# Two taps in one VectorE product, and a scaling moved to ScalarE, in the last phase of an SSM-convolution and gated-MLP training step

## The chip, the cores and the metric

The kernel runs on one core of a Trainium2 chip. The metric is device time in microseconds of one execution; lower is better. Of the kernel before, three runs were timed and one more was profiled.

## The reference

The forward pass normalizes x (2048 rows of 512), and adds three things: x itself, a long convolution gated by xn, and a bilinear MLP. The outputs are the forward result and all gradients:

```python
xn = (x - mean) / sqrt(var + 1e-5)
k_shift = sum(k_pad[:, t:t+S] * shift_k[:, 3 - t] for t in range(4))
kv = k_shift * v
y = irfft(rfft(kv) * rfft(ssm_k)) + kv * ssm_D
out_0 = x + xn * y + (xn @ w_gate * (xn @ w_up)) @ w_down
```

Three of the outputs matter here. `out_0` is the forward result. `out_1` is the gradient of x: with dxn the gradient that reaches xn, it is `rstd * (dxn - mean(dxn) - xn * mean(dxn * xn)) + grad_out`. `out_2` is the gradient of k, four shifted copies of the gradient of k_shift, each times one tap of shift_k, summed.

## The kernel before, in words

The 2048 rows lie as 128 partitions times 16 rows, so a block of two rows per partition is a tile of 128 x 2 x 512. The first phases do the MLP forward and backward by chunks of 256 rows, and the convolution as a staged Fourier transform through DRAM buffers. The last phase starts at about 315 us. Its main loop is `dw()` (line 1020): for each of eleven blocks of 128 hidden columns, TensorE turns the hidden values round (`hid_t`, line 846), and forms the weight gradients (`pd`, line 1002, and `pu`, line 1038). ScalarE copies the results out of PSUM: `nath` and `natd` from the transposes, `og` and `od` from the products. PSUM has three buffers of two banks (pool `ps2`, shared by pt, pu, pq, pk, po) and two small ones (pool `ps1`).

Between the steps of `dw()` four side jobs advance, each by its own start and step (line 1165): `inv_y` (the last inverse transform, which yields y and the gradient of k_shift, `dks`), `dsk_gram` (the tap gradient: TensorE products `pk`, VectorE masks `kd`), `inv_dk` (the gradient of ssm_k: `po`, `o5t`, which needs four loads `g` from DRAM, line 785) and `ew`, which runs the list `tail`.

`tail` holds, for b from 0 to 7, `final(b)` and one step later `bwd(b - 1)`. `final(b)` (line 1104) loads the next block `bb`, then writes `out_0` (o: a product, line 1112, a sum, line 1113, and the store, line 1114), and the norm gradient: `e` (line 1116), `dxn` with its two sums (lines 1120 and 1121), the two means (1122, 1123), `dxn + xn * m2` (1126), the scaling `e = dxn * rstd + m1` (1127), the sum with grad_out (1128) and the store of `out_1` (1129). All of it is on VectorE, and the stores are in SyncE's queue. `bwd(b)` (line 1083) writes `out_2`: four products with one tap each (1091 and 1093) and three sums (1094), on VectorE, and a store (1095).

Buffers: pool `c2` has one buffer for each name and `c2b` has two. So `o`, `e` and `dxn` have one buffer, which is written again one call later; `dk` and `bb` have two. `tk`, the temporary of `bwd`, shares the buffer of `dxn` (`tag="dxn"`). `dxn` is float32, 4 KB a partition; `tk` is bfloat16, 2 KB.

What sets the order: the code is traced, and a planner then writes the order of each engine's queue. It takes the place in the trace as an instruction's rank and its own table of costs for when inputs are there; blocks in `tc.high_priority(offset=SOON)` get a rank 300 earlier. On the chip each engine and each DMA queue takes its instructions in that order, and each waits for its inputs and for the readers of the buffer that it writes. Almost all loads and stores of this phase are issued by SyncE's one queue.

Of the kernel before, what the change touches and what calls it, by code (L numbers as in the profile page):

```python
# [8 lines left out]
BF = mybir.dt.bfloat16  # L9
F32 = mybir.dt.float32  # L10
I32 = mybir.dt.int32
ALU = mybir.AluOpType
ACTF = mybir.ActivationFunctionType
# [5 lines left out]
D = 512  # L19
F = 1376  # L20
R = 16
P = 128
# [168 lines left out]
def kernel(  # L191
# [24 lines left out]
    nc = tc.nc  # L216
    from concourse.masks import make_identity

    def nat(ap):
        return ap.rearrange("(p r) d -> p r d", r=R)  # L220
# [5 lines left out]
    o0_n = nat(out_0[0])  # L226
# [35 lines left out]
    skb = const.tile([P, 4, D], BF, name="skb")  # L262
    mv = const.tile([P, R, 2], F32, name="mv")
    rstd = const.tile([P, R], F32, name="rstd")
# [618 lines left out]
    for tag in mainit:  # L883
        if tag == "wa":
            wa_es.close()
            c1 = ctx.enter_context(tc.tile_pool(name="c1", bufs=1, reuse_waits="tile"))
            xnC = c1.tile([P, R, D], BF, name="xnC")
# [17 lines left out]
    c2 = ctx.enter_context(tc.tile_pool(name="c2", bufs=1, side="right", reuse_waits="tile"))  # L905
    yC = c2.tile([P, R, D], BF, name="yC")
    dks = c2.tile([P, R + 3, D], BF, name="dks")
    s1 = c2.tile([P, R], F32, name="s1")
    s2 = c2.tile([P, R], F32, name="s2")
    m1 = c2.tile([P, R], F32, name="m1")  # L910
# [172 lines left out]
    def bwd(b):  # L1083
        rb = slice(2 * b, 2 * b + 2)
        dk = c2b.tile([P, 2, D], BF, name="dk")
        t = c2.tile([P, 2, D], BF, name="tk", tag="dxn")
        for j in range(4):
            src = dks[:, 2 * b + j:2 * b + j + 2, :]
            w = skb[:, j:j + 1, :].to_broadcast((P, 2, D))
            if j == 0:  # L1090
                nc.vector.tensor_tensor(dk[:], src, w, op=ALU.mult)
            else:
                nc.vector.tensor_tensor(t[:], src, w, op=ALU.mult)  # L1093
                nc.vector.tensor_tensor(dk[:], dk[:], t[:], op=ALU.add)
        nc.sync.dma_start(o2_n[:, rb, :], dk[:])

    FL = {}
# [1 line left out]
    def load_fin(b):  # L1099
        bb = c2b.tile([P, 2, 2, D], BF, name="bb")  # L1100
        nc.sync.dma_start(bb[:], BX[:, 2 * b:2 * b + 2, :, :])
        FL[b] = bb

    def final(b):
        if b + 1 < 8:
            load_fin(b + 1)
        bb = FL.pop(b)
        rb = slice(2 * b, 2 * b + 2)
        tt = nc.vector.tensor_tensor
        stt = nc.vector.scalar_tensor_tensor  # L1110
        o = c2.tile([P, 2, D], BF, name="o0")
        tt(o[:], xnC[:, rb], yC[:, rb], op=ALU.mult)
        tt(o[:], o[:], bb[:, :, 0, :], op=ALU.add)
        nc.sync.dma_start(o0_n[:, rb, :], o[:])
        e = c2.tile([P, 2, D], BF, name="e")
        tt(e[:], goC[:, rb], yC[:, rb], op=ALU.mult)
        dxn = c2.tile([P, 2, D], F32, name="dxn")
        for i in range(2):
            r = 2 * b + i
            stt(dxn[:, i], e[:, i], 1.0, bb[:, i, 1, :], op0=ALU.mult, op1=ALU.add, accum_out=s1[:, r:r + 1])  # L1120
            stt(e[:, i], dxn[:, i], 1.0, xnC[:, r, :], op0=ALU.mult, op1=ALU.mult, accum_out=s2[:, r:r + 1])  # L1121
        nc.vector.tensor_scalar(m2[:, rb], s2[:, rb], -1.0 / D, None, op0=ALU.mult)
        stt(m1[:, rb], s1[:, rb], -1.0 / D, rstd[:, rb], op0=ALU.mult, op1=ALU.mult)
        for i in range(2):
            r = 2 * b + i
            stt(dxn[:, i], xnC[:, r, :], m2[:, r:r + 1], dxn[:, i], op0=ALU.mult, op1=ALU.add)  # L1126
            nc.vector.tensor_scalar(e[:, i], dxn[:, i], rstd[:, r:r + 1], m1[:, r:r + 1], op0=ALU.mult, op1=ALU.add)
        tt(e[:], e[:], goC[:, rb], op=ALU.add)
        nc.sync.dma_start(o1_n[:, rb, :], e[:])

# [15 lines left out]
    for b in range(8):  # L1146
        tail.append(lambda b=b: final(b))
        if b > 0:
            tail.append(lambda b=b: bwd(b - 1))
    tail.append(lambda: bwd(7))  # L1150

    def ew():
# [51 lines left out]
```

## Time and profile before

| what | value |
|---|---|
| three runs, us | 486.96, 488.27, 490.54 (median 488.27) |
| the profiled execution, us | 485.82 |
| its span, us | 484.1 |
| TensorE's last matmul starts, us | 480.2 |
| VectorE's last sum of `bwd` ends, us | 470.2 |
| granted TensorE clock | 1.0 |

In the profile, PE is TensorE's matmuls, PEld its weight loads, DVE VectorE, ACT ScalarE, SP SyncE, and SPq the queue of DMA issues on SyncE. A group of instructions is shown with its line, engine, operation, output and inputs, shapes, count, then busy us and mean ns, then the idle time of the engine ahead of them and what ended it. A row of the timeline has the start in us from the span's start, the length in us, the engine, the line, the operation, and a count where several are merged. A wait has who waited, for whom, then us in total, times, and the longest.

### The profile page before, as it was taken

Reading aid. Unit: us, or ns where it says so; the run is one execution under the profiler, and the core shown is the slowest. Engines: PE = TensorE matmul, PEld = TensorE weight load, DVE = VectorE, ACT = ScalarE, POOL = GpSimd, SP = SyncE. Lnnn points to the kernel's source line nnn. Section 1 sums busy time; section 2 is a strip of 40 time slices with the busy share of each in tenths; the row PEclk is TensorE's granted clock in tenths of the full one; section 3 lists DMA queues with packets and bytes.
Section 4 is the critical chain, followed back from the end, with each engine's and each line's share of the span. In section 5 each row is a group of like instructions: output and inputs, shape, how many; then the busy total and the mean of one; then the engine's idle time right before and its main releaser. Section 6 shows DMA issues by size and latency. Waiting matters only on the chain.

```text
span 484.1 us, 10517 instructions
## 1 busy us (share of the span) xinstructions
PE 470.3 (97%) x4335; PEld 313.7 (65%) x4335; DVE 340.6 (70%) x622; ACT 318.2 (66%) x354; POOL 15.3 (3%) x31
## 2 busy tenths in 40 slices
PE   7998999999999999999999999999999999999977
PEld 6866754647638547447447744567777788777775
DVE  7889969988274768667686865013276899999780
ACT  4976896759658678779779974466577524543141
POOL 8010000000000000000000000020000000000000
PEclk9999999999999999999999999999999999999999
DMA  8999998999997965978968298999999979699747
GB/s 269 374 379 359 294 263 313 349 308 338 310 303 277 252 220 196 295 251 254 301 214 258 78 334 294 399 327 307 321 396 384 367 263 404 203 254 245 209 149 246
DMA packets 105469, 139.87 MB, mean 289 GB/s; under 512 B 33323, under 2 KB 78800, under 8 KB 103758
## 3 DMA queue, kind: packets, MB, share of 16 engines
q1 hardware_dynamic: 103838, 137.84, 86.1%
q10 hardware_dynamic: 1584, 1.36, 1.0%
q8 instruction: 34, 0.56, 0.5%
q14 instruction: 13, 0.11, 0.1%
HBM read 68.45 MB, written 63.41 MB: 272 GB/s over the span
## 4 chain that ended last, share of the span: by engine, by line
PE 61%; DVE 21%; DMA 13%; issue 2%; ACT 2%; SPq 0%; DVEq 0%; ACTq 0%
PE px L553 16%; PE pgu L510 13%; PE py L546 8%; PE pdh L516 6%; PE pu L1038 5%; DMA out_dram<-o 4%; PE pf L368 3%; PE pg L611 3%; PE ps L582 3%; PE pd L1002 2%; DMA HDD<-hd 2%; DVE dxn L1126 2%; DVE tk L1093 2%; DVE dxn L1120 2%; DVE e L1121 2%
## 5 line engine op out<-in xcount | busy, mean ns | idle before, releaser
L553 PE MATMUL px<-WT,hd 128*128 128x512 bf16 (+1 forms) x352 | 81.0, 380 | 0.0
L1038 PEld LDWEIGHTS <-xnC 128*128 128x128 bf16 x704 | 67.1, 98 | 8.8 <-issue 0.9
L553 PEld LDWEIGHTS <-hd 128*128 128x128 bf16 (+1 forms) x352 | 32.8, 98 | 44.4 <-issue 7.5
L1038 PE MATMUL pu<-natd,xnC 128*128 128x256 bf16 x512 | 58.5, 273 | 0.2 <-ACT nath L235 0.2
L235 ACT CAST GO<-pg 128x1024 bf16<-128x1024 f32 x48 | 46.3, 1017 | 12.8 <-PE pg L611 6.6
L235 ACT CAST SP<-ps 128x1024 bf16<-128x1024 f32 x48 | 46.6, 1029 | 11.9 <-PE ps L582 10.9
L510 PE MATMUL pgu<-xt,Wu 128*128 128x256 bf16 (+1 forms) x352 | 53.2, 273 | 0.6 <-DVE fst L238 0.4
L235 ACT CAST gu<-pgu 128x1024 bf16<-128x1024 f32 (+1 forms) x48 | 45.4, 947 | 12.3 <-PE pgu L510 11.9
L510 PE MATMUL pgu<-xt,Wg 128*128 128x256 bf16 (+1 forms) x352 | 52.8, 273 | 0.2 <-DMA Wg<-in_B_w_gate_dram 0.2
L598 DVE TENSOR_TENSOR T<-SP 128x2048 bf16<-128x2048 bf16 x24 | 29.4, 1223 | 30.8 <-ACT SP L235 30.8
L516 PE MATMUL pdh<-gt,WdT 128*128 128x256 bf16 (+1 forms) x352 | 47.1, 273 | 0.1
L510 PEld LDWEIGHTS <-Wu 128*128 128x128 bf16 (+1 forms) x352 | 32.9, 100 | 14.7 <-issue 10.2
L546 PE MATMUL py<-Wd,hd 128*128 128x512 bf16 (+1 forms) x176 | 41.4, 380 | 0.0
L235 ACT CAST og<-pu 128x1024 bf16<-128x1024 f32 (+1 forms) x11 | 10.9, 994 | 46.2 <-PE pu L1038 25.6
L235 ACT CAST fst<-pf 128x1024 bf16<-128x1024 f32 x40 | 39.1, 1034 | 0.8 <-ACT dh L235 0.5
L235 ACT COPY natd<-pt 128x2048 bf16<-128x2048 bf16 x16 | 30.0, 1876 | 13.5 <-PE pt L846 13.5
L516 PEld LDWEIGHTS <-WdT 128*128 128x128 bf16 (+1 forms) x352 | 34.9, 100 | 5.2 <-issue 0.2
L510 PEld LDWEIGHTS <-Wg 128*128 128x128 bf16 (+1 forms) x352 | 34.8, 100 | 4.1 <-DMA Wg<-in_B_w_gate_dram 0.5
L530 DVE TENSOR_TENSOR hd<-gu 128x512 bf16<-128x512 bf16 (+1 forms) x48 | 19.1, 398 | 19.0 <-ACT gu L235 19.0
L531 DVE TENSOR_TENSOR hd<-gu,dh 128x1024 bf16<-128x1024 bf16 (+1 forms) x48 | 30.8, 642 | 1.0
L1002 PE MATMUL pd<-goC,nath 128*128 128x512 bf16 x128 | 30.1, 379 | 0.0
L546 PEld LDWEIGHTS <-hd 128*128 128x128 bf16 (+1 forms) x176 | 16.4, 98 | 20.7 <-issue 3.3
(171 smaller groups left out, 698.0 us busy)
## 6 DMA issues: line engine op xcount, KB each, us to landing
HDD<-hd SPq DMA_DIRECT2D x35, 384.0 KB, 3.6
FD<-fst SPq DMA_DIRECT2D x24, 512.0 KB, 4.5
X<-FD SPq DMA_DIRECT2D x24, 512.0 KB, 4.7
GD<-GO SPq DMA_DIRECT2D x24, 512.0 KB, 3.9
g<-GD SPq DMA_DIRECT2D x12, 1024.0 KB, 7.9
hb<-HDD SPq DMA_DIRECT2D x8, 1344.0 KB, 8.5
bb<-BX SPq DMA_DIRECT2D x8, 512.0 KB, 6.9
BX<-bx SPq DMA_DIRECT2D x7, 512.0 KB, 3.6
```

Source lines behind the costliest of these rows:

```text
L235: nc.scalar.copy(o, i)
L368: nc.tensor.matmul(pf[:, c, :], lhsT=TB.W1[:, c, :], rhs=src[:, i, :], start=True, stop=not point)
L510: nc.tensor.matmul(pgu[:w, i, t, :], lhsT=W[:, c, f0:f0 + w], rhs=xt[:, :, c, :], start=(c == 0), stop=(c == NC4 - 1))
L516: nc.tensor.matmul(pdh[:w, i, :], lhsT=WdT[:, c, f0:f0 + w], rhs=gt[:, :, c, :], start=(c == 0), stop=(c == NC4 - 1))
L530: nc.vector.tensor_tensor(hd[:fw, fb0:fb0 + n, 0, :], gu[:fw, :n, 0, :], gu[:fw, :n, 1, :], op=ALU.mult)
L531: nc.vector.tensor_tensor(hd[:fw, fb0:fb0 + n, 1:3, :], gu[:fw, :n], dh[:fw, :n].unsqueeze(2).to_broadcast((fw, n, 2, 256)), op=ALU.mult)
L546: nc.tensor.matmul(py[:], lhsT=hd[:fw, fb, 0, ss], rhs=Wd[:fw, fb, :], start=(fb == 0), stop=(fb == NFB - 1))
L553: nc.tensor.matmul(px[:], lhsT=hd[:fw, fb, t, ss], rhs=W[:fw, fb, :], start=(t == 1 and fb == 0), stop=(t == 2 and fb == NFB - 1))
L582: nc.tensor.matmul(ps[32 * q:32 * q + 32, a, :], lhsT=TB.EF[64 * a:64 * a + 64, 4 * g + q, ri].rearrange("p k j -> p (k j)"), rhs=X[64 * a ...
L598: tt(W[:].rearrange("p c a d -> p c (a d)"), A[:, i:i + 1].rearrange("p c a d -> p c (a d)").to_broadcast((P, 2, 2 * D)), B[:].rearrange(" ...
L1002: nc.tensor.matmul(pd[:fw, :], lhsT=nat_h(fb, r), rhs=goC[:, r, :], start=(r == 0), stop=(r == R - 1))
L1038: nc.tensor.matmul(pu[:, c, :, :fw], lhsT=xnC[:, r, cs(c)], rhs=nat_d(fb, r), start=(r == 0), stop=(r == R - 1))
```

## The change

In `bwd`, a product now takes two taps at once: its input is three rows of `dks` read as two overlapping pairs of rows (four rows in the pattern, one of them twice), its output is a tile of 128 x 2 x 2 x 512 bfloat16, 4 KB a partition like `dxn`. Two such products replace four. There are still three sums: the first adds the two halves of the first product into `dk`, the other two add the halves of the second. All products now write `t`, the first one too, which before wrote `dk`.

In `final`, the scaling of the norm gradient is an activation on ScalarE (Identity, with a scale and a bias from a column of `rstd` and `m1` each), two per call. `out_0`'s product, sum and store stand behind these two, ahead of the sum with grad_out; before they stood first.

```diff
     def bwd(b):
         rb = slice(2 * b, 2 * b + 2)
         dk = c2b.tile([P, 2, D], BF, name="dk")
-        t = c2.tile([P, 2, D], BF, name="tk", tag="dxn")
-        for j in range(4):
-            src = dks[:, 2 * b + j:2 * b + j + 2, :]
-            w = skb[:, j:j + 1, :].to_broadcast((P, 2, D))
-            if j == 0:
-                nc.vector.tensor_tensor(dk[:], src, w, op=ALU.mult)
-            else:
-                nc.vector.tensor_tensor(t[:], src, w, op=ALU.mult)
-                nc.vector.tensor_tensor(dk[:], dk[:], t[:], op=ALU.add)
+        t = c2.tile([P, 2, 2, D], BF, name="tk", tag="dxn")
+        for j in (0, 2):
+            s = dks[:, 2 * b + j:2 * b + j + 3, :]
+            (part, row, elem) = s.ap
+            src = bass.AP(s.tensor, s.offset, [part, [row[0], 2], [row[0], 2], elem])
+            w = skb[:, j:j + 2, :].unsqueeze(2).to_broadcast((P, 2, 2, D))
+            nc.vector.tensor_tensor(t[:], src, w, op=ALU.mult)
+            nc.vector.tensor_tensor(dk[:], t[:, 0] if j == 0 else dk[:], t[:, 1 if j == 0 else 0], op=ALU.add)
+            if j:
+                nc.vector.tensor_tensor(dk[:], dk[:], t[:, 1], op=ALU.add)
         nc.sync.dma_start(o2_n[:, rb, :], dk[:])
...
-        o = c2.tile([P, 2, D], BF, name="o0")
-        tt(o[:], xnC[:, rb], yC[:, rb], op=ALU.mult)
-        tt(o[:], o[:], bb[:, :, 0, :], op=ALU.add)
-        nc.sync.dma_start(o0_n[:, rb, :], o[:])
         e = c2.tile([P, 2, D], BF, name="e")
...
             stt(dxn[:, i], xnC[:, r, :], m2[:, r:r + 1], dxn[:, i], op0=ALU.mult, op1=ALU.add)
-            nc.vector.tensor_scalar(e[:, i], dxn[:, i], rstd[:, r:r + 1], m1[:, r:r + 1], op0=ALU.mult, op1=ALU.add)
+            nc.scalar.activation(e[:, i], dxn[:, i], ACTF.Identity, bias=m1[:, r:r + 1], scale=rstd[:, r:r + 1])
+        o = c2.tile([P, 2, D], BF, name="o0")
+        tt(o[:], xnC[:, rb], yC[:, rb], op=ALU.mult)
+        tt(o[:], o[:], bb[:, :, 0, :], op=ALU.add)
+        nc.sync.dma_start(o0_n[:, rb, :], o[:])
         tt(e[:], e[:], goC[:, rb], op=ALU.add)
         nc.sync.dma_start(o1_n[:, rb, :], e[:])
```

## The prediction

> **What bounds the kernel now.** I read the page first, then busy time by stretch for the last phase (from about 315 us), the waits, the chain of work that ended last, and the timelines of TensorE, VectorE and ScalarE side by side. The page and the stretches:
>
> ```profile
> PE 470.3 (97%) x4335; PEld 313.7 (65%) x4335; DVE 340.6 (70%) x622; ACT 318.2 (66%) x354; POOL 15.3 (3%) x31
> ```
>
> ```profile
> 380.00:400.00 20.00, 20.00 (x221) 15.63 (x220) 19.09 (x40) 8.02 (x6) 0.00 (x0) 1.00 0.86 315
> 400.00:420.00 20.00, 20.00 (x225) 15.75 (x223) 19.51 (x46) 9.84 (x8) 0.00 (x0) 1.00 0.88 329
> 440.00:460.00 20.00, 19.98 (x179) 14.92 (x176) 17.13 (x41) 4.96 (x7) 0.00 (x0) 1.00 0.88 215
> 460.00:484.00 24.00, 17.94 (x182) 15.45 (x182) 10.12 (x16) 6.95 (x9) 0.00 (x0) 1.00 0.57 198
> ```
>
> Columns: stretch, length, busy time of PE, PEld, DVE, ACT, POOL, granted clock, DMA share, GB/s. TensorE is never idle from 340 to 440 at full clock, VectorE is over 95% busy from 380 to 420, ScalarE half busy. So the last phase has two full engines, of which TensorE sets the end: VectorE's last sum ends at 470.2, TensorE's last matmul at 480.6. What TensorE loses in this phase stands in the waits and in the chain:
>
> ```profile
> DVE dk L1091 <- DMA out_dram<-dk: 2.7, 1, 2.7
> PE po L977 <- DMA g<-GD: 2.7, 1, 2.7
> PE pu L1038 <- ACT nath L235: 0.2, 1, 0.2
> ```
>
> ```profile
> 455.21 0.33 SPq L1095
> ...
> 456.73 5.89 DMA g<-GD
> 462.62 0.04 issue
> 462.67 1.07 PE po L977 x16
> ```
>
> The only two losses are 0.2 and 2.7 us. The 2.7 is the last g load: SyncE issued it at 456.7, behind a dk store (L1095) that waited for VectorE. VectorE is late, and by how much the timelines tell:
>
> ```profile
> 403.55 1.94 PE L1061 MATMUL pk<-khC,dks 128*64 128x256 bf16 x32
> 409.01 1.94 PE L1061 MATMUL pk<-khC,dks 128*64 128x256 bf16 x32
> 434.54 0.22 PE L993 MATMUL ptd<-ident,dDs 128*4 128x128 bf16 x1
> ```
>
> ```profile
> 410.17 0.86 DVE L1067 TENSOR_TENSOR kd<-pk,ident 64x256 f32<-64x256 f32 x2
> 416.01 0.86 DVE L1067 TENSOR_TENSOR kd<-pk,ident 64x256 f32<-64x256 f32 x2
> 443.29 0.21 DVE L238 COPY dDt<-ptd 4x128 bf16<-4x128 bf16 x1
> ```
>
> kd is written with high priority, so the planned order has it right behind its matmuls; it runs 4.7 us (405.49 to 410.17) and 5.1 us (410.95 to 416.01) behind them. The two earlier kd pairs, by the same rows, are 2.8 and 3.5 us behind; dDt, of ordinary priority, 8.5. VectorE falls ever further behind the order that all queues were written in. That backlog is the number this forecast turns on.
>
> **The change part by part.** The rows for its prices:
>
> ```profile
> L1094 DVE TENSOR_TENSOR dk<-dk,tk 128x1024 bf16<-128x1024 bf16 x24 | 16.6, 692 | 0.7
> L1093 DVE TENSOR_TENSOR tk<-dks,skb 128x1024 bf16<-128x1024 bf16 x24 | 16.5, 689 | 0.5
> L1127 DVE TENSOR_SCALAR e<-dxn,rstd,m 128x512 bf16<-128x512 f32 x16 | 8.1, 541 | 0.0
> L598 DVE TENSOR_TENSOR T<-SP 128x2048 bf16<-128x2048 bf16 x24 | 29.4, 1223 | 30.8 <-ACT SP L235 30.8
> ```
>
> ```profile
> L331 ACT ACTIVATE rstd<-mv,eps_t 128x2 f32<-128x2 f32 x8 | 2.4, 298 | 11.7 <-DVE mv L325 11.7
> L76 ACT ACTIVATE zf<-ti 128x1024 bf16<-128x1024 int32 x1 | 1.1, 1072 | 0.0
> L76 ACT ACTIVATE iwf<-tiv 128x256 f32<-128x256 int32 x1 | 0.4, 402 | 0.0
> ```
>
> *Products for two taps.* Per `bwd`, four products of 1024 elements (4 x 0.69) become two of 2048; three sums stay. L598 has the size, two bf16 inputs and a repeated operand: 1.22 us. Saved: 4 x 0.689 - 2 x 1.223 = 0.31 us, 2.5 us over eight calls. The overlapping read has no row. The good end is L598. For the bad end take the float32 rate: L1067 (256 elements, 0.42) and L1120 (512, 0.69) give 1.04 ns an element, so 2048 take 2.28 us and the eight calls lose 14.4 us. I take L598, since L531, whose operand is also repeated through a middle dimension, runs 1024 in 0.64. No TensorE instruction waits for `dk`.
>
> *Scaling to ScalarE.* VectorE loses 16 operations; in the chain a pair takes 0.92, so 7.4 us over eight calls. ScalarE gains 16. From the rows, (1.072 - 0.402)/768 = 0.87 ns an element and 0.30 of fixed cost with a pointer bias, so 0.74; a second pointer adds about what the first does, 0.10 (0.298 against 0.199 for dDs, a copy of 4 elements without one): 0.84. The low end is a plain 128x512 copy of ScalarE (od, 0.59), the high end the whole fixed cost again, 1.04. I take 0.84: 13.4 us more on an engine with 2.7 to 8.1 us of idle time ahead of most `og` copies. The function is Identity, which this kernel has not used: a table load took 1.28 us in the three places where Sin and Sqrt brought one, and none stands in front of the copies. I take none; the high end is one, 1.3 us on TensorE if it meets a full queue. The Trainium skill (ScalarE: Activation LUTs, Table sets: the hidden batching unit) has identity in every set as filler; by that the high end falls away and the sum stays.
>
> *New waits.* VectorE's `e + goC` waits for both scalings; `out_0`'s product and sum (1.3 us) stand there to cover them. The second scaling ends about 1.0 us after the second L1126 (2 x 0.84 - 0.66), so the cover holds if ScalarE is free, and fails by up to 1.9 us if a `nath` or `natd` copy (1.88 each) has just begun. `tk` shares dxn's one buffer, so the products of `bwd` also wait for ScalarE; before, j = 0 wrote `dk` directly and could run early. And `e`'s first product now leads `final`: its buffer waits for the store of the last `e`, which lands in 2.6 to 6.7 us (median 4.7), with only `bwd` (4.6 us) between: 0 to 2.1 us each time, where before `out_0`'s two operations stood in front. I take 0.4 us per call for the three, 3.2 in all, against 9.9 saved: VectorE is some 6.7 us shorter.
>
> *Moved `out_0`.* Two operations and one 256 KB store per call (L1114, 0.35 us of SyncE's queue, landing 3.3). The store goes from about 5 us ahead of `e`'s store to about 1 us; its reader of the buffer comes one full call later as before: nothing. POOL's queue is not touched.
>
> *What reaches TensorE.* Gain: VectorE is earlier, so the dk store ahead of the last g load goes earlier by more than 2.7 us; that wait goes, and so may the 0.2. Next late would be nothing on TensorE before 480.6, so the gain ends at 2.9 us. Loss: ScalarE's queue is in order, and behind each scaling stand the copies that empty PSUM for TensorE. The order is planned with VectorE on time; where VectorE is 3 to 8 us behind, ScalarE stands still for that time. Whether TensorE feels it depends on the place. Ahead of `og` there are gaps of 8.1 us (414.6), 4.7 (430.3) and 2.7 (443.1), where it costs nothing. Around a `nath`, `natd` pair there is no slack: the 0.2 us wait at 422.7 on `nath` is TensorE needing the buffer at once, with three buffers turning over within 3 us. Once TensorE has lost that time, it is no longer ahead of VectorE by as much, so the loss is not paid eight times; the total is about the largest backlog that meets such a place. I take one such meeting at 5.1 us of backlog with 1.2 us absorbed: 3.9 us.
>
> Sum, against the profiled execution (485.82 us with a span of 484.1): -2.7 - 0.2 + 3.9 = +1.0, so 486.8. The median of the runs shown, 488.27, is 2.45 above that execution; on it the forecast is 489.3.
>
> **Rivals.**
> *No meeting: a small gain.* All scalings fall into idle gaps; TensorE loses nothing new and the g load comes in time: 485.82 - 2.9 = 482.9, on the median 485.4. For it speak ScalarE's 50% idle time and 9.9 us of relief on VectorE; against it, a `nath`/`natd` pair every 16 us and eight calls. 28 in 100.
> *ScalarE's queue is the new brake: slower.* The scaling of one of the last two or three calls stands ahead of the copies with the full backlog of 8.5 us (dDt) and little slack: TensorE loses 8.3 or, with the stores of `e` also late, up to 11, less 2.7: +5.6 to +8.3, 493.9 to 496.6. It decides from a TensorE loss of 7.6 us on. Against it: the late calls meet ScalarE at its emptiest (5.0 us busy of 20). 16 in 100.
> *The wide product runs at the float32 rate.* VectorE gets 14.4 - 7.4 = 7 us longer instead of shorter, the backlog passes to TensorE: about +8, 496. 4 in 100.
> *The scaling was cheaper on VectorE.* A pair costs ScalarE 1.68 us and VectorE 0.92; if a copy of 1.88 has begun ahead of it each time and `out_0` fails as cover, VectorE loses 8 x 1.9 = 15 for 9.9 gained, the g load comes 5 us later and TensorE with it: 490.8, 493.3 on the median. Against it, ScalarE waits for VectorE's backlog and so is mostly free. 5 in 100. The Trainium skill (ScalarE: Activation LUTs, Rules for kernel authors) points this way: it sends multiplication and addition to VectorE, not ScalarE.
>
> **How the numbers follow.** The forecast, one meeting of 2 to 7 us (487.4 to 492.4 on the median): 45 in 100; 2 are left for what I have not seen, below 483. About 1% (4.9 us) is what a measurement of this kernel can tell from no change. Slower: 16 of the queue, 4 of the float32 rate, half of the 5, less 2 for the edge of the queue's case: 0.20. Faster: the 2, and 2 of the small gain, since TensorE's waits hold only 2.9 us in all: 0.04. Within: 0.76. The range leaves out about 9 below 484.5 (the lower third of the small gain, with the spread of the runs, and the 2) and 9 above 495.5 (the upper part of the queue's case and most of the float32 rate).
>
> **What would show it.** Right: the scaling on ScalarE at about 0.84 us; products of 128x2048 at 1.22; no wait of `po` on g<-GD; one or two waits of `pu`, `pq` or `po` on ACT `nath`, `natd` or `og` of some 4 us in all, and ScalarE idle ahead of a scaling, released by DVE dxn L1126. Wrong: TensorE waits of over 7 us or none; products over 1.3 us; VectorE idle ahead of `e + goC` by over 0.5 us a call; a late g, hb or natT load in the chain.

## The result, and the profile after

| | before | after |
|---|---|---|
| median of the runs timed side by side, us | 487.72 (6 runs) | 494.86 (6 runs, 492.16 to 497.09) |
| ratio, 95% interval | | 1.0134 [1.0092, 1.0176] |
| the profiled execution, us | 485.82 | 495.94 |
| its span, us | 484.1 | 494.1 |
| mean granted TensorE clock | 1.0 | 0.993 |
| VectorE's last sum of `bwd` ends, us | 470.2 | 475.4 |

The kernel became 1.3% slower. The time lies inside the range (484.5 to 495.5), but 5.6 us above the value named, and on the side that had got a chance of 0.20. That it lies inside is in part luck: the sum was made on the profiled execution, and there the range ends at 495.5 - 2.45 = 493.05, while the one after took 495.94.

First the page of the kernel after, in its line of busy times, and busy time by stretch. The columns are those of the prediction: PE, PEld, DVE, ACT, POOL, clock, DMA share, GB/s.

```profile
PE 470.1 (95%) x4293; PEld 315.7 (64%) x4335; DVE 332.2 (67%) x590; ACT 328.8 (67%) x370; POOL 15.3 (3%) x31
```

```profile
400.00:420.00 20.00, 18.54 (x221) 15.24 (x221) 19.01 (x45) 8.41 (x7) 0.00 (x0) 1.00 0.99 380
...
460.00:494.00 34.00, 25.77 (x233) 20.59 (x231) 14.38 (x25) 10.86 (x14) 0.00 (x0) 0.95 0.52 172
```

VectorE has 8.4 us less to do (340.6 before), ScalarE 10.6 more (318.2), and TensorE as much as before. But TensorE, idle for only 0.2 us from 340 to 440 before, now has holes (18.54 us busy of 20, and at the end 25.77 of 34, where it was 17.94 of 24), and at the end its clock is below 1. What the holes wait for stands in the waits of the last phase (who waited, for whom: us in total, times, longest):

```profile
ACT e L1124 <- DVE dxn L1123: 30.5, 6, 8.7
DVE e L1129 <- ACT e L1124: 7.9, 8, 1.6
DVE e L1113 <- DMA out_dram<-e: 6.2, 2, 4.4
...
PE po L977 <- ACT o5t L235: 4.6, 1, 4.6
PE pq L919 <- ACT nath L235: 2.4, 1, 2.4
```

Line 1124 is the scaling, now on ScalarE, 1123 the operation ahead of it on VectorE (1126 before), 1129 the sum with grad_out, 1113 `e`'s first product. The wait of `po` for the last g load (2.7 us before) is gone, as forecast. In its place TensorE waits for ScalarE's copies out of PSUM: the 4.6 and 2.4 us shown, 1.0 of `pk` for `natd`, 0.5 of `pu` for `nath` and 0.2 of `pd` for `nat`, some 8.8 us. And ScalarE stands still for 30.5 us at a scaling whose `dxn` VectorE has not written yet. The two belong together, as ScalarE's timeline shows at the costliest place (start, length, line, operation, and in brackets the idle time ahead of it):

```profile
463.79 1.52 ACT L1124 ACTIVATE e<-dxn,m,rstd 128x512 bf16<-128x512 f32 x2 [8.74 <-DVE dxn L1123]
...
465.68 1.01 ACT L235 CAST o5t<-po 128x1024 bf16<-128x1024 f32 x1
```

ScalarE does nothing for 8.74 us, then two scalings, and then four copies (`od`, `o5t`, `nat`, `og`, of which one is shown) run one right behind another: their PSUM tiles had been full, and they stood behind the scaling in the queue. TensorE at the same place and at the first such place, in call 1:

```profile
378.00 0.59 PE L919 MATMUL pq<-g,IW 128*128 128x512 bf16 x1 [2.43 <-ACT nath L235]
...
466.74 1.86 PE L977 MATMUL po<-IW,g 128*128 128x128 bf16 x16 [4.64 <-ACT o5t L235]
```

The sixteen `po` matmuls at 466.74 take 1.86 us; the same group took 1.07 in the kernel before, at 462.67. Stretches of 2 us tell why, here those of the first hole (columns as above):

```profile
376.00:378.00 2.00, 0.00 (x1) 0.00 (x0) 1.77 (x2) 2.00 (x3) 0.00 (x0) 0.99 0.97 239
378.00:380.00 2.00, 1.78 (x4) 0.66 (x5) 1.93 (x3) 1.76 (x2) 0.00 (x0) 0.50 0.97 269
380.00:382.00 2.00, 2.00 (x10) 1.00 (x9) 1.43 (x3) 1.32 (x2) 0.00 (x0) 0.66 1.03 397
```

The granted clock falls to 0.50 for some 3.4 us, by which 2 x (1 - 0.50) + 2 x (1 - 0.66) = 1.7 us of TensorE's work is lost. Behind the hole before 466.74 the clock is 0.67, 0.50 and 0.97 in the stretches from 466, 468 and 470, which takes the same 1.7.

The account, on the spans of the two profiled executions (484.1 and 494.1): waits for ScalarE 8.8, less the 2.9 us of waits that went, plus twice 1.7 of clock: 9.3 of the 10.0 us. The other 0.7 is not assigned to a place (0.6 us of TensorE's waits are put down to "issue"). The medians are 7.1 us apart, not 10.0. The profiled execution of the kernel before happened to have a clock of 1.0, but the mean over its 90 runs in the experiments below is 0.9973, and over the six runs after the change 0.9945. So on average the change costs some 1.4 us of clock, an estimate from these means, and with the 5.9 us of waits that makes 7.3.

The prices of the two new forms, from the groups (count, then busy us and mean ns of one, then the idle time ahead of them):

```profile
L1092 DVE TENSOR_TENSOR tk<-dks,skb 128x2048 bf16<-128x2048 bf16 x16 | 19.5, 1221 | 0.3
L1124 ACT ACTIVATE e<-dxn,m,rstd 128x512 bf16<-128x512 f32 x16 | 12.3, 809 | 36.1 <-DVE dxn L1123 30.5 <-issue 5.6
```

The wide product takes 1.221 us and the scaling 0.809; no table load stands ahead of a scaling.

### The profile page after: what moved, and what is told of

It reads as the page before. It is cut to its first block, busy times and chain, and to the rows that moved or that the text cites. A ratio compares the mean times of both kernels' runs of the same rounds, so it can differ in the third digit from the quotient of the medians.

```text
span 494.1 us, 10463 instructions
## 1 busy us (share of the span) xinstructions
PE 470.1 (95%) x4293; PEld 315.7 (64%) x4335; DVE 332.2 (67%) x590; ACT 328.8 (67%) x370; POOL 15.3 (3%) x31
## 4 chain that ended last, share of the span: by engine, by line
PE 67%; DMA 13%; DVE 12%; ACT 4%; issue 3%; SPq 1%; ACTq 0%; DVEq 0%
PE px L553 14%; PE pgu L510 13%; PE pu L1038 9%; PE py L546 7%; PE pdh L516 6%; PE pd L1002 4%; PE pg L611 3%; PE ps L582 3%; DMA out_dram<-e 3%; DMA hb<-HDD 2%; PE pt L846 2%; PE pq L919 2%; PE pf L368 2%; DMA HDD<-hd 2%; DMA x_b<-in_A_q_dram 2%
## 5 line engine op out<-in xcount | busy, mean ns | idle before, releaser
L553 PE MATMUL px<-WT,hd 128*128 128x512 bf16 (+1 forms) x338 | 78.3, 379 | 1.8 <-issue 1.6
L598 DVE TENSOR_TENSOR T<-SP 128x2048 bf16<-128x2048 bf16 x24 | 29.4, 1224 | 30.7 <-ACT SP L235 30.7
L546 PE MATMUL py<-Wd,hd 128*128 128x512 bf16 (+1 forms) x169 | 40.3, 380 | 0.6 <-issue 0.3
L1124 ACT ACTIVATE e<-dxn,m,rstd 128x512 bf16<-128x512 f32 x16 | 12.3, 809 | 36.1 <-DVE dxn L1123 30.5
L531 DVE TENSOR_TENSOR hd<-gu,dh 128x1024 bf16<-128x1024 bf16 (+1 forms) x48 | 30.8, 643 | 1.0
L598 DVE TENSOR_TENSOR U<-SP 128x2048 bf16<-128x2048 bf16 x24 | 29.3, 1219 | 0.0
```

The lines of the kernel that those rows point to most:

```text
L531: nc.vector.tensor_tensor(hd[:fw, fb0:fb0 + n, 1:3, :], gu[:fw, :n], dh[:fw, :n].unsqueeze(2).to_broadcast((fw, n, 2, 256)), op=ALU.mult)
L546: nc.tensor.matmul(py[:], lhsT=hd[:fw, fb, 0, ss], rhs=Wd[:fw, fb, :], start=(fb == 0), stop=(fb == NFB - 1))
L553: nc.tensor.matmul(px[:], lhsT=hd[:fw, fb, t, ss], rhs=W[:fw, fb, :], start=(t == 1 and fb == 0), stop=(t == 2 and fb == NFB - 1))
L598: tt(W[:].rearrange("p c a d -> p c (a d)"), A[:, i:i + 1].rearrange("p c a d -> p c (a d)").to_broadcast((P, 2, 2 * D)), B[:].rearrange(" ...
```

## The experiments

The theory: ScalarE's in-order queue, standing still at a scaling that VectorE has not yet fed, holds back the copies that empty PSUM, and TensorE pays. The rivals: VectorE is late because it now waits for ScalarE and for the store of `e`; ScalarE has too much to do; the moved `out_0` or the wide product costs. The table has all runs; "TensorE for ScalarE" is the sum of TensorE's waits for ScalarE from 340 us on, in the profiled execution.

| kernel | median, us | ratio to before | 95% | TensorE for ScalarE, us | mean clock |
|---|---|---|---|---|---|
| after | 494.86 | 1.0134 | 1.0092 to 1.0176 | 8.8 | 0.993 |
| e1 new bwd alone | 486.59 | 0.9958 | 0.9927 to 0.9989 | 0.2 | 0.996 |
| e2 new final alone | 491.07 | 1.0060 | 1.0019 to 1.0101 | 6.4 | 1.000 |
| e3 scaling back on VectorE | 487.89 | 0.9992 | 0.9961 to 1.0023 | 0.2 | 0.999 |
| e4 out_0 first again | 492.99 | 1.0107 | 1.0049 to 1.0166 | 6.9 | 0.996 |
| e5 scaling on GpSimd | 488.01 | 1.0003 | 0.9978 to 1.0029 | 0.2 | 0.999 |
| e6 two buffers for e | 489.48 | 1.0039 | 1.0009 to 1.0068 | 4.2 | 0.999 |
| e7 ScalarE in calls 0, 2, 4, 5, 6 | 487.22 | 1.0002 | 0.9970 to 1.0033 | 2.2 | 1.000 |
| e8 ScalarE in calls 1, 3, 7 | 493.35 | 1.0097 | 1.0059 to 1.0135 | 3.9 | 0.993 |
| e9 new bwd alone, stores on GpSimd's queue | 507.89 | 1.0409 | 1.0381 to 1.0437 | 0.2 | 0.983 |
| e10 new bwd alone, hb loads on GpSimd's queue | 502.03 | 1.0292 | 1.0232 to 1.0351 | 0.2 | 0.993 |
| e11 new bwd alone, two buffers for o | 484.53 | 0.9940 | 0.9910 to 0.9971 | 0.2 | 0.999 |
| e12 scaling a step later | 494.37 | 1.0147 | 1.0121 to 1.0173 | 8.3 | 0.997 |

**The two halves, e1 and e2.** e1 has the kernel before with only the new `bwd`, e2 with only the new `final`.

> The two-tap products alone; final is as before, with the scaling on VectorE. Theory (the scaling in ScalarE's queue holds up the PSUM copies): no new wait of TensorE; VectorE 2.5 us shorter; the wait on the last g load shrinks from 2.7 to 0 to 2.7 us: ratio to the kernel before 0.994 to 1.000. Rival (VectorE became the brake through tk's shared, wider buffer): slower, 1.005 or more, with TensorE waits behind VectorE.

> The change in final alone (scaling on ScalarE, out_0 behind it); bwd is as before. Theory: most of the loss is here, ratio 1.008 to 1.02, with ScalarE idle ahead of the scaling for over 20 us in all and TensorE waits of several us on ScalarE copies. Rival (the loss is made by the products of bwd and tk's buffer): 1.000 or less.

The wide product gains 0.4%, the new `final` loses 0.6%. In e1 the g wait is gone, and one thing is late next, in the waits of TensorE:

```profile
PE pt L846 <- DMA hb<-HDD: 2.1, 1, 2.1
```

In e2 the waits are those of the kernel after, without any new `bwd` (the largest, of 6.4 us in all):

```profile
PE pq L919 <- ACT nath L235: 2.3, 1, 2.3
```

So the loss starts in `final`, but its ratio is under the expected 1.008, and the halves do not add up: 0.9958 x 1.0060 is 1.0018, against 1.0134 for both together. By the profiles, the whole has what e2 lacks: 2.4 us more of waits for ScalarE, the two drops of the clock, and VectorE's 6.2 us of waits for the stores of `e`, of which e2 has none. Ahead of the scaling of call 6 ScalarE stands still for 8.17 us in the whole and for 5.31 in e2. Why the stores of `e` are waited for only when the wide products are there too was not followed.

**The scaling back on VectorE, e3; out_0 first again, e4; the scaling on GpSimd, e5.** Each undoes one thing of the whole change.

```diff
e3
-            nc.scalar.activation(e[:, i], dxn[:, i], ACTF.Identity, bias=m1[:, r:r + 1], scale=rstd[:, r:r + 1])
+            nc.vector.tensor_scalar(e[:, i], dxn[:, i], rstd[:, r:r + 1], m1[:, r:r + 1], op0=ALU.mult, op1=ALU.add)
e4: the four lines of o stand ahead of e's tile, as before the change
e5
-            nc.scalar.activation(e[:, i], dxn[:, i], ACTF.Identity, bias=m1[:, r:r + 1], scale=rstd[:, r:r + 1])
+            nc.gpsimd.tensor_scalar(e[:, i], dxn[:, i], rstd[:, r:r + 1], m1[:, r:r + 1], op0=ALU.mult, op1=ALU.add)
```

> The whole change but for one thing: the scaling goes back to VectorE; out_0 still stands behind it and the products are wide. Theory: the loss is gone, ratio 0.993 to 1.002. Rival (the moved out_0, that is e first and its wait for the store of the last e, makes VectorE late): still slower, 1.006 or more, with waits of e's first product on its store of 5 us or more in all.

> The whole change but for the move: out_0's product, sum and store stand first in final as before, the scaling is on ScalarE. Theory (queue): the loss stays, 1.008 to 1.02, and VectorE's sum with grad_out waits 1 to 2 us a call for ScalarE, or bwd's. Rival (the moved out_0 is the cause): 1.002 or less.

> The whole change, but the scaling is a tensor_scalar on GpSimd, in whose queue nothing of the last phase stands behind it. VectorE still gives the work away and still waits for another engine to give it back. Theory (the loss is ScalarE's queue standing still ahead of the PSUM copies): the loss is gone, ratio 0.993 to 1.003, no TensorE wait on ScalarE over 0.5 us. Rival (the loss is the round trip itself: VectorE waiting for the scaling and for the store of e, and so late): still slower, 1.006 or more.

With the scaling off ScalarE the loss is gone (0.9992 and 1.0003); with it there, and `out_0` in its old place, the loss stays (1.0107). e5 is the sharper of the two, since VectorE is relieved and waits for another engine just as in the kernel after. Its waits:

```profile
POOL e L1124 <- DVE dxn L1123: 124.3, 9, 35.5
DVE e L1129 <- POOL e L1124: 10.4, 8, 1.4
```

VectorE waits 10.4 us for the scaling, longer than the 7.9 for ScalarE; the engine that scales stands still for 124 us. Nothing stands behind it in GpSimd's queue that TensorE needs, and TensorE waits for ScalarE no more than before the change (0.2 us; it waits 2.1 us for VectorE instead). The rival "VectorE's wait for the scaling costs the time" falls.

**What feeds the standstill, e6.** `e` gets two buffers in the kernel after, so that its first product does not wait for the store of the last call.

```diff
-        e = c2.tile([P, 2, D], BF, name="e")
+        e = c2b.tile([P, 2, D], BF, name="e")
```

> The whole change with two buffers for e, so that e's first product doesn't wait for the last store of out_1. Theory: in the changed kernel this wait (6.2 us in all, 4.4 of it ahead of call 6) makes VectorE late and so ScalarE's standstill longer; without it the standstill ahead of calls 6 and 7 shrinks by some 4 us and TensorE's 4.6 us wait with it: ratio 1.002 to 1.010. Rival (the backlog has other sources, or other waits take its place): 1.010 or more as in the changed kernel.

About two thirds of the loss go (1.0134 to 1.0039; the intervals do not meet). ScalarE's standstill falls from 30.5 us to

```profile
ACT e L1124 <- DVE dxn L1123: 18.7, 6, 6.5
```

Some idle time ahead of scalings is put down to "issue" instead (6.4 us here, 5.6 in the kernel after); with it the fall is from 36.1 to 25.1. In call 7 TensorE waits 1.1 us for `o5t` instead of 4.6, and its waits for ScalarE fall from 8.8 to 4.2 in all; the clock does not drop in this execution. These 4.6 us and the 3.4 of the clock make up the 8.0 between the spans (494.1 and 486.1).

The expectation was met in its number, but not in its way. It meant the wait ahead of call 6, and that one stayed (4.43 us before the edit, 4.21 with two buffers); only the 1.73 ahead of call 7 went. The planner also placed a few ScalarE operations otherwise, and TensorE's wait in call 1 moved to another copy (2.1 us for `yC`). So how much of the 0.0095 comes from the buffer is open. What the pair shows is that in call 7 a shorter standstill (8.74 us, then 6.44) goes with a shorter wait of TensorE (4.64, then 1.12). That the change itself makes part of VectorE's lateness stands in the chain of the kernel after (start, length, what):

```profile
437.08 8.56 DMA out_dram<-e
...
454.75 4.08 DMA out_dram<-e
...
458.85 0.69 DVE e L1113
```

Two stores of `e` are in the chain of work that ended last. The second, issued at 454.75, is under way for 4.08 us and holds back the next call's first product; the scaling of that call starts at 463.79, and the copies behind it end the hole in TensorE.

**Number or place, e7 and e8.** The scaling is on ScalarE in some calls only, in the others on VectorE.

```diff
-            nc.scalar.activation(...)
+            if b in (0, 2, 4, 5, 6):   # e8: (1, 3, 7)
+                nc.scalar.activation(...)
+            else:
+                nc.vector.tensor_scalar(...)
```

> The whole change, with the scaling on ScalarE in calls 0, 2, 4, 5 and 6 alone, on VectorE in 1, 3 and 7. In the changed kernel the TensorE waits stood behind calls 1, 3 and 7 (2.4, 1.3 and 4.6 us). Theory (the place in ScalarE's queue decides, not the number): most of the loss is gone, 0.995 to 1.006. Rival (each call costs its share): five eighths of the loss stay, 1.007 to 1.010.

> The counterpart: the scaling on ScalarE in calls 1, 3 and 7 alone. Theory (place): most of the loss is here, 1.006 to 1.014, with TensorE waits behind the same three calls. Rival (number): three eighths of it, 1.002 to 1.005.

Five calls cost nothing (1.0002), three cost 1% (1.0097). The longest standstill ahead of a scaling in all these profiles lies in e7; ScalarE's timeline:

```profile
419.27 1.52 ACT L1125 ACTIVATE e<-dxn,m,rstd 128x512 bf16<-128x512 f32 x2 [11.22 <-DVE dxn L1123]
```

It is 11.22 us long, and all of TensorE's waits for ScalarE in e7 make 2.2. In e8 one of 3.02 us, at 375.38, is followed by this in TensorE's timeline, and by 0.74 us more for `natd` at 380.46:

```profile
378.70 1.02 PE L919 MATMUL pq<-g,IW 128*128 128x512 bf16 x4 [2.15 <-ACT nath L235]
```

Of 3.02 us of standstill right ahead of a `nath`, `natd` pair, TensorE loses 2.9; of 8.15 us ahead of the scaling at 459.97 in the same kernel it loses 0.5. The place in ScalarE's queue decides, not the number of scalings nor the length of the standstill. (In e8's profile call 3 costs 0.3 us and call 7 0.5, so the three calls do not pay alike; its clock drops twice, once far ahead of the change, see the last section.) The rival "too much work on ScalarE" falls with it: e7 has the more of it.

**Two attempts on the late hb load, e9 and e10: misses.** In e1 SyncE issued that load 0.4 us behind a store of `e` that had waited 6.0 us for VectorE. e9 sends the stores of `o`, `e` and `dk` through GpSimd's queue (`nc.gpsimd.dma_start`), e10 the hb loads after the second.

> The two-tap products alone, and the 24 stores that wait for VectorE (o, e, dk) issued by GpSimd's queue, so that no load for TensorE stands behind VectorE in SyncE's queue. If what is left of TensorE's waits (2.7 us on g before, 2.1 us on hb with the two-tap products) is SyncE's queue standing still behind VectorE, both go: ratio 0.990 to 0.996, below the two-tap products alone. Rival (the loads are late because the transfers themselves are slow there, or GpSimd's issues cost more): 0.996 or more.

> The two-tap products alone, and the hb loads after the second issued by GpSimd's queue, where nothing stands ahead of them. The load that TensorE waited 2.1 us for was issued 0.4 us behind a store of e for which SyncE had waited 6.0 us. Theory (SyncE's queue behind VectorE): the wait on hb goes, ratio 0.991 to 0.996. Rival (the 1.3 MB behind the 2 MB of khC is slow wherever it is issued): 0.996 or more, the wait stays.

Both became much slower (1.0409, 1.0292). The waits of e9:

```profile
DVE e L1117 <- DMA out_dram<-e: 18.3, 5, 4.9
PE pt L846 <- DVE kd L1067: 10.1, 3, 5.6
```

In e10 the same two are 24.5 and 12.3 us. The wait for hb itself, 2.1 us in e1, is 0.5 in e9 and gone in e10. But VectorE waits longer, for the stores of `e` (2.5 us in e1) and in e10 also for a load `bb` (17.7 us, 7.9 in e1); it falls back, and then its own reads of PSUM (`kd`) hold TensorE: the pattern seen on ScalarE. With the queue the written order of the engines changed too, so these runs do not say what a store on GpSimd's queue costs by itself.

**The late load from the other side, e11.** `o` gets two buffers in e1's kernel (`o = c2b.tile(...)`), since VectorE waited 6.8 us for its stores there.

> The new bwd alone (scaling and out_0 as before), and o, out_0's tile, gets two buffers instead of one. With the new bwd alone VectorE waited 6.8 us for o's stores (three times, longest 4.5), and TensorE 2.1 us for a late hb load, which SyncE issued behind a store of e that waited 6.0 us for VectorE. Theory (the late hb load comes from VectorE's lateness, part of which is its wait for o's buffer): that wait goes, the store of e and the hb load behind it go earlier, TensorE's 2.1 us shrink to under 0.5, and the ratio to the kernel before is 0.988 to 0.994, under the 0.996 of the new bwd alone. Rival (VectorE was idle there for longer than it cost, or another late store takes its place): ratio 0.994 to 1.000, with a TensorE wait of 1.5 us or more on a load or on VectorE.

The 2.1 us wait for hb is gone: in TensorE's waits from 340 us on, only the 0.2 us of `pu` for `nath` is left, as in the kernel before. The ratio, 0.9940, lies on the border of the two expectations. The profile bears the theory out, and the span follows: e1's 485.1 less the 2.1 of the wait, and less up to 1.7 for the half clock that came behind it in e1 (last section), gives 481.3 to 483.0; it is 482.4. Against e1 the intervals overlap, so that it beats the kernel before is shown, and that it beats e1 is not.

**The scaling a step later, e12: a miss.** The two scalings, and `out_0` and the sum with them, come one entry of `tail` later.

```diff
+    def scale(b):
+        (rb, bb, e, dxn) = FE.pop(b)
...
-        tail.append(lambda b=b: final(b))
+        tail.append(lambda b=b: (scale(0) if b == 1 else None, final(b)))
         if b > 0:
-            tail.append(lambda b=b: bwd(b - 1))
+            tail.append(lambda b=b: (scale(b), bwd(b - 1)))
```

> The whole change, but the two scalings, out_0 and the sum of a call come one entry of the tail later (ahead of bwd of the block before), so that in ScalarE's written order the scaling stands two to five copies further back; the work is the same. Theory (the loss is ScalarE standing still at a scaling that VectorE has not fed yet, with PSUM copies behind it): ScalarE's idle time released by dxn falls from 30.5 us to under 12, TensorE's waits for ScalarE from some 9 us to under 2.5, and the ratio to the kernel before is 0.990 to 1.004. Rival (13 us more on ScalarE, or the sum and the store that wait for it, cost the time wherever the scaling stands): ratio 1.007 to 1.02, with TensorE waits of 4 us or more. One place gets worse in either case: e of the second call now has its product right behind the store of the first.

The waits:

```profile
ACT e L1132 <- DVE dxn L1124: 31.9, 5, 8.1
DVE o L1134 <- DMA out_dram<-o: 15.3, 1, 15.3
PE pu L1038 <- ACT og L235: 4.6, 1, 4.6
```

The standstill did not shrink, so the edit did not do what it was made for. `out_0` moved along, its first two calls came into adjacent entries of `tail`, and with one buffer VectorE stood 15.3 us for the first store of `o` (in the chain it is under way for 12.43 us, from 367.28): the scalings stand later in ScalarE's queue, and VectorE is later too. The ratio and TensorE's waits for ScalarE (8.3 us) are those that the rival named. But since the standstill was not shortened, the run does not decide between the two: TensorE again pays behind a standstill, and whether a later place alone would be free stays open.

## Why the prediction was right or wrong

*The products for two taps: price right.* 1.221 us each, as taken from L598; the overlapping read costs nothing beside it. (The 0.64 us quoted for L531 is a mean with eight shorter operations; its 1024 elements take 0.688.) The groups of `bwd` sum to 38.5 us before and to 36.0 in e1, the 2.5 forecast. VectorE's busy time, which counts overlapping records once, fell by only 1.2 us (340.6 to 339.4): the relief of the engine was half of what the prices say.

*The scaling on ScalarE: right.* 0.809 us for the 0.84 taken; VectorE lost 7.2 us in e2 (340.6 to 333.4) for the 7.4 taken. The table load at the high end did not come, as the Trainium skill (ScalarE: Activation LUTs, Table sets: the hidden batching unit) has it for identity.

*The moved out_0: nothing that these runs can tell.* With it first again the ratio is 1.0107 against 1.0134, and the intervals overlap.

*The gain: right.* The 2.7 us wait for g went. "Next late would be nothing on TensorE" held only by half: in e1, without the loss, hb was late next, by 2.1 us.

*The new waits on VectorE: wrong.* "0.4 us per call for the three, 3.2 in all": VectorE waits 7.9 us for the scalings and 6.2 for the stores of `e` (0.6 before), together some 13.5 more. The 7.9 are 1.0 us a call ahead of the sum with grad_out, over the 0.5 that the prediction named as a sign of being wrong. In the sum they were only set against what VectorE saves. The account that fits is that they bring back the backlog of which the loss is made: two stores of `e` lie in the chain that ended last. How much they make of it is not shown: e6 took away a third of the waits for `e`'s stores, ScalarE's standstill fell by 11 us and the ratio by 0.0095, but other things moved too.

*The loss: right in kind, wrong in size. This is the term that failed.* The prediction had the mechanism, the engine and the copies, and priced "one such meeting at 5.1 us of backlog with 1.2 us absorbed: 3.9 us". There were three: 2.4 us in call 1, 1.3 in call 3 (0.98 for `natd` and 0.32 for the `nath` next to it), 4.6 in call 7. It argued that TensorE, once it has lost time, is no longer ahead of VectorE by as much, so that the loss is paid about once. But VectorE lost time as well, by its new waits; in call 7, the last, ScalarE stood still for 8.74 us, longer than in any other. And the prediction had no term for the clock, which adds 3.4 us in the profiled execution, and on average, by the means above, some 1.4. With 8.8 + 3.4 for 3.9 its sum is -2.9 + 12.2 = +9.3, that is 495.1 on its profiled execution, which took 495.94 after the change.

*The backlog was read from the less telling rows.* `kd`'s distance behind `pk` was 5.1 us before. After the change the four `kd` pairs are 1.9, 2.9, 1.6 and 1.6 us behind, and ScalarE still stood still for 7.59 us ahead of the scaling at 420.79. So a result with high priority need not show how late the operations of ordinary priority are. `dDt`, 8.5 us behind before and after, is near the standstills of calls 4, 6 and 7 (7.59, 8.17 and 8.74 us); that it tells them in general is not shown by one row.

*The rivals.* The time is that of "ScalarE's queue is the new brake" (493.9 to 496.6), and so is the deciding point: TensorE's loss of 8.8 us is over the 7.6 named. Its way is only half of what came: the last call did it, but calls 1 and 3 paid too. It had got 16 in 100, because the late calls meet ScalarE at its emptiest. That was the error behind the chance: 8.74 us of standstill need no busy engine, only a copy behind them that TensorE waits for. "The scaling was cheaper on VectorE" was right in that VectorE waits about 1 us a call, and e5 shows that such a wait, at 1.3 us a call, leaves the kernel at the time of before. Against the rule of the Trainium skill that went with it (ScalarE: Activation LUTs, Rules for kernel authors) no run speaks: with the scaling on VectorE the kernel is faster (e3 against after), though for the queue and not for the price of an operation.

## What to carry to other kernels

Before an operation is moved to an engine with idle time, look at what stands behind its new place in that engine's queue: if those are copies that empty PSUM, the price is not the operation's 0.8 us but what TensorE has to wait for these copies while the operation's input is late: 2.9 of 3.02 us at one place of e8, 0.5 of 8.15 at another. Look for that lateness in operations of the same priority as its input, and ask whether the change brings it back, by a new wait or a buffer written again sooner. An idle engine on whose queue nothing critical waits (GpSimd here) can take the operation: here without a loss against the kernel before, and without a gain.

## What was not expected of the hardware

*The clock halves after short holes.* In e1 TensorE was idle for 2.06 us, up to 386.88, and then ran at half clock for some 3.4 us. In e8 a hole of 1.47 us far ahead of the change was enough. The stretch of 1 us in e1, then the hole and the stretch in e8:

```profile
387.00:388.00 1.00, 1.00 (x11) 1.00 (x10) 0.96 (x6) 0.00 (x0) 0.00 (x0) 0.50 0.98 393
...
41.98 1.18 PE L413 MATMUL ptk<-ident,ssk 128*128 128x128 bf16 x16 [1.47 <-DVE fst L238]
44.00:45.00 1.00, 1.00 (x7) 0.74 (x5) 1.00 (x2) 1.00 (x1) 0.00 (x0) 0.50 0.50 190
```

A hole of 1.47 to 1.69 us stands at this place in all fourteen profiles, the one before included, and the clock dropped behind it in e8 alone. Of the eight holes of 2 to 3 us three were followed by half clock (2.06 in e1, 2.43 after the change, 2.15 in e8 with another of 0.74 close behind) and five were not (2.69 before, 2.66 in e3, 2.28 in e2, 2.12 in e6, 2.51 in e10). All seven over 3 us were (4.64 after, 3.99 in e4, 4.62 in e12, 4.56, 5.63 and 3.19 in e9, 7.95 in e10). So in these runs it can happen from 1.5 us on, and always did over 3. The Trainium skill (TensorE: Matmul & The Clock Gate, What's actually happening) describes an idle window of about 3.4 us that runs freely, with half clock after at least one idle window. The 3.4 us of half clock agree with its window; the drops after 2.06 and 1.47 us of idle do not agree with a whole idle window. A hole that drops the clock costs 1.7 us on top of its length, which nearly doubles the price of a wait of 2 us.

*GpSimd as a scaling engine.* The same scaling, 128x512 from float32 to bfloat16 with two pointers, takes 942 ns there (e5), 809 on ScalarE and 541 on VectorE.
